# The first products of a GEGLU layer: three blocks of x by one transposing transfer, gate rows on ScalarE's queue

## The chip, the cores and the metric

The kernel runs on one core of a Trainium2 chip. The metric is the device time of one execution in microseconds, the median over runs; lower is better. The engines of the core are TensorE (PE, matrix products; PEld is its loading of weights), VectorE (DVE), ScalarE (ACT), GpSimd (POOL) and SyncE (SP). SyncE and ScalarE issue the transfers of this kernel, each on a queue of its own; sixteen DMA engines carry them.

## The reference

```python
B, S, D, F = 32, 32, 1024, 3584
# x [32, 32, 1024], w_gate and w_up [1024, 3584], w_down [3584, 1024], all bfloat16

def reference(x, w_gate, w_up, w_down):
    return (_gelu(x @ w_gate) * (x @ w_up)) @ w_down
```

`_gelu` is the tanh form of GELU. With x flattened, N = 1024 tokens go through a hidden width of F = 3584.

## The kernel before

A tile of 128 rows or columns is called a block. D has eight blocks (`DT`), F has 28 (`FT`), and tokens come in two halves of `NB` = 512. The eight blocks of D are cut in two halves of `KD` = 4, and these in two of `KQ` = 2. Both layers are computed by a scheme with seven products of half-sized matrices in place of eight, with sums and differences of quarters (`sums`, `t1` to `t4`) made on GpSimd and VectorE.

The quarter product that needs no sums is computed first, ahead of the rest, for 24 blocks of F (`NAHEAD`): the second half of x's columns times the lower half of the gate weights. Its moving operand is `b21` (x transposed: four blocks of D on the partitions, 512 tokens of the first half). Its weights come in six tiles `a12_ahead[i]`, each with four rows (blocks of D, index k) and four blocks of F (`KB`, index j). Tiles 0 and 1 are called a12a in the profile, tiles 2 to 5 a12b. A product for (i, j) sums over the four k into one accumulator of 128x512 in PSUM; `product_ahead` issues the matmuls for a range of k (line 290 in the profile). The finished accumulators are copied into `ahead_at` by ScalarE and VectorE (L348, L305).

Everything from `tc.manual_schedule()` on (line 191) is in an order written out by hand: each engine runs its instructions in the order of the code, and the tool that builds the kernel adds the waits. Transfers raise completion counters, eight of them used in turn; a transfer that reuses a counter waits for its previous user.

How x gets into `b21` is what the change is about. x lies in memory with tokens as rows, and `b21` needs it transposed:

- Block 0 of the four is loaded plainly into `x_nat` by SyncE (`load_nat`, L193), transposed on TensorE in four pieces (L266, function `transposed`), and copied from PSUM into `b21` by VectorE (L271).
- Block 1 is loaded plainly by ScalarE's queue and takes the same way through TensorE, between the products.
- Blocks 2 and 3 come by one transposing transfer on SyncE's queue (`load_xT`, L213). GpSimd's copy of one element (L221) from `x_nat` into `b21` is put ahead of it; the transfer overwrites that element, and so waits for the copy and with it for `x_nat`.

The rows of gate weights are issued by `load_ahead` (L206). On SyncE: row 0 of tile 0, row 0 of tile 1, rows 2 and 3 of tile 0 together, and, behind the transposing transfer, rows 2 and 3 of tile 1 together. On ScalarE: row 1 of tile 0 and row 1 of tile 1, behind a small read (`probe`, L202) and block 1 of x. After these SyncE issues tiles 2 and 3, the first chunks of the up and gate weights (L136), tile 4, the first half of x for both halves of the tokens, tile 5, and the last quarter of x.

TensorE starts with six products of constants (L254, `NWARM`), then transposes block 0 (L266), runs seven small products of constants (L275, `NFILL`), and then the products of tiles 0 and 1: row 0 of tile 0 in halves of 256 tokens (`by_halves(0)`), the transposes of block 1, row 0 of tile 1 for three of its four j, row 1 of tile 0 in halves, the remaining rows 0 and 1 of tile 1, and then rows 2 and 3 of both tiles, with the copies. Tiles 2 to 5 follow by `group_ahead`. Chunks of F (`for ci in range(NCH)`) and then the second layer take up the rest of the time.

Of the kernel before, what the change touches and what calls it, by code (L numbers as in the profile page):

```python
# [13 lines left out]
def kernel(  # L14
# [20 lines left out]
    nc = tc.nc  # L35
    P = nc.NUM_PARTITIONS
    fp32 = mybir.dt.float32
    f32r = mybir.dt.float32r
    bf16 = mybir.dt.bfloat16
# [3 lines left out]
    xf = x.flatten_outer_dims()  # L43
# [3 lines left out]
    NB = 512  # L47
    assert N == 2 * NB and D == 2 * NB and F % (4 * P) == 0
    DT, FT = D // P, F // P
    KD = DT // 2  # L50
# [4 lines left out]
    KQ = DT // 4  # L55
# [4 lines left out]
    KB = 4  # L60
# [12 lines left out]
    spool = one.enter_context(tc.tile_pool(name="s", bufs=2))  # L73
    xpool = one.enter_context(tc.tile_pool(name="x", bufs=1))
    ework = one.enter_context(tc.tile_pool(name="ework", bufs=2))
    ps1 = ctx.enter_context(tc.tile_pool(name="ps1", bufs=2, space=bass.MemoryType.PSUM))
# [29 lines left out]
    BANKS = {"A": 6, "C": 2}  # L106

    def acc(tag):
        return ps1.tile([P, NB], fp32, name=f"ps{tag}", tag=tag, bufs=BANKS[tag])
# [5 lines left out]
    b21 = xpool.tile([P, KD, NB], bf16, name="b21")  # L115
# [68 lines left out]
    ident = xpool.tile([P, P], bf16, name="ident")  # L184
    make_identity(nc, ident)
    NB_P = NB // P
    probe = xpool.tile([P // 4, KD, 2], bf16, name="probe")
    HALF = NB_P // 2
    x_nat = spool.tile([P, NB_P, KQ * P], bf16, name="x_nat", tag="s1")

    with tc.manual_schedule():
        def load_nat(eng, dt, p0, p1):
            eng.dma_start(  # L193
                out=x_nat[:, p0:p1, dt * P : (dt + 1) * P],
                in_=xf[p0 * P : p1 * P, (KD + dt) * P : (KD + dt + 1) * P].rearrange("(b p) d -> p b d", p=P),
            )

        assert KQ == 2
        load_nat(nc.sync, 0, 0, NB_P)


        nc.scalar.dma_start(out=probe, in_=wg_r[::4, KD:, :2])  # L202

        def load_ahead(i, k0, k1, eng=nc.sync, j0=0, j1=KB):
            f0 = i * KB
            eng.dma_start(  # L206
                out=a12_ahead[i][:, k0:k1, j0 * P : j1 * P],
                in_=wg_r[:, KD + k0 : KD + k1, (f0 + j0) * P : (f0 + j1) * P],
            )

        def load_xT(nb, d0, d1):
            t = ((b11, b12), (b21, b22))[d0 // KD][nb]
            nc.sync.dma_start_transpose(  # L213
                out=t[:, d0 % KD : (d1 - 1) % KD + 1, :], in_=xf[nb * NB : (nb + 1) * NB, d0 * P : d1 * P]
            )

        load_ahead(0, 0, 1)
        load_nat(nc.scalar, 1, 0, NB_P)
        load_ahead(1, 0, 1)
        load_ahead(0, KQ, KD)  # L220
        nc.gpsimd.tensor_copy(b21[:1, KQ, :1], x_nat[:1, 0, :1])  # L221
        load_xT(0, KD + KQ, DT)
        load_ahead(0, 1, KQ, nc.scalar)
        load_ahead(1, 1, KQ, nc.scalar)
        a12_ahead += [spool.tile([P, KD, KB * P], bf16, name="a12b", tag=t) for t in ("s2", "s4", "s1", "s3")]
        load_ahead(1, KQ, KD)
        def load_halves(i):
# [5 lines left out]
        for which in (1, 0):  # L233
            load_w_all(0, which)
        load_ahead(4, 0, KD)
        load_xT(0, 0, KD)
        load_xT(1, 0, KD)
        for j0 in range(0, KB, KB // 2):
            load_ahead(5, 0, KD, j0=j0, j1=j0 + KB // 2)
# [13 lines left out]
        for _ in range(NWARM):  # L253
            nc.tensor.matmul(warm_ps, lhsT=ones_w, rhs=ones_m, start=True, stop=True)  # L254

        def tp_tile(cols):
            return ps1.tile([P, cols], bf16, name="tp", tag="A", bufs=BANKS["A"])

        tps = [[tp_tile(HALF * P) for _ in range(2)]]
        whole_tp = tp_tile(NB_P * P)  # L260
        tps.append([whole_tp[:, h * HALF * P : (h + 1) * HALF * P] for h in range(2)])

        def transposed(dt):
            for half, tp in enumerate(tps[dt]):
                for b in range(HALF):
                    nc.tensor.transpose(  # L266
                        tp[:, b * P : (b + 1) * P], x_nat[:, half * HALF + b, dt * P : (dt + 1) * P], ident
                    )
            for half, tp in enumerate(tps[dt]):
                p0 = half * HALF * P  # L270
                nc.vector.tensor_copy(b21[:, dt, p0 : p0 + HALF * P], tp)  # L271

        transposed(0)
        for _ in range(NFILL):
            nc.tensor.matmul(warm_ps[:, :P], lhsT=ones_w, rhs=ones_w, start=True, stop=True)  # L275

# [11 lines left out]
        def product_ahead(ps, i, j, k0=0, k1=KD, cols=slice(None)):  # L288
            for k in range(k0, k1):
                nc.tensor.matmul(  # L290
                    ps[:, cols],
                    lhsT=a12_ahead[i][:, k, j * P : (j + 1) * P],
                    rhs=b21[:, k, cols],
                    start=(k == 0 and not cols.start),
                    stop=(k == KD - 1),
                    skip_group_check=True,
                )
# [32 lines left out]

        both = (nc.scalar.copy, nc.vector.tensor_copy)
        ps = [[acc(t) for t in tags] for tags in ("CCAA", "AAAA")]
        def by_halves(k):
            for half in range(2):
                for j in range(KB):
                    product_ahead(ps[0][j], 0, j, k, k + 1, slice(half * HALF * P, (half + 1) * HALF * P))

        by_halves(0)
        transposed(1)
        for j in range(KB - 1):  # L340
            product_ahead(ps[1][j], 1, j, 0, 1)
        by_halves(1)
        for j in range(KB):
            product_ahead(ps[1][j], 1, j, 0 if j == KB - 1 else 1, KQ)
        for i in (0, 1):
            for j in range(KB):
                product_ahead(ps[i][j], i, j, KQ)
# [26 lines left out]
        for ci in range(NCH):  # L374
# [7 lines left out]
            s1, s2, s3, s4 = ([s[:, :, fl * P : (fl + 1) * P] for fl in range(len(fts))] for s in s_tiles[ci])  # L382
# [87 lines left out]
        def halves(name, tags, dtype):  # L470
            return [late.tile([P, QF, NB], dtype, name=name, tag=t) for t in tags]

        def parts(two):

            return [two[b // 2][:, k0 % QF : (k1 - 1) % QF + 1, :] for b, (k0, k1) in enumerate(batches)]
# [15 lines left out]
        s1 = parts(halves("s1d", ("slo", "shi"), f32r))  # L491
# [103 lines left out]
        for h0, h1, upto in ((0, NB - P, NB - P), (NB - P, NB, NB)):  # L595
            cols = slice(h0, h1)
            ps = acc("C")[:, : h1 - h0]
# [33 lines left out]
```

## Time and profile before

| what | value |
|---|---|
| median of 3 runs | 273.57 us (272.9 to 273.75) |
| profiled execution, its own time | 273.33 us |
| profiled execution, span from first to last instruction | 271.4 us |
| mean granted TensorE clock | 1.000 |
| first transposing transfer: issue, landing after it | 3.44 us, 4.1 us |
| x's first and second block: landing after issue | 2.4 us, 3.3 us |
| gate rows of tiles 0 and 1, single: landing after issue | 3.1 to 3.8 us |
| first product of a gate row (L290) | 4.67 us on the chain |

Times inside the execution are microseconds from the start of the span. The chain of waits follows the work that ended last back to the start: at each step to what released it, or to the instruction before it on its engine. The timeline lists instructions in order of time, several of one line merged into one row ("x6"). A row "SPq" or "ACTq" is the issue of a transfer on SyncE's or ScalarE's queue; the time from its start to the landing of the data stands with the transfers. In a window's row the busy time of each engine is followed by granted clock, the share of the DMA engines' time and the rate in GB/s.

### The profile page before, as it was taken

How to read it: one execution, taken by the hardware profiler on the slowest of the kernel's cores; microseconds unless marked ns; L12 is line 12 of the kernel's file. 1: busy time of each engine (PE TensorE's matmuls, PEld its weight loads, DVE VectorE, ACT ScalarE, POOL GpSimd, SP SyncE). 2: the span in 40 equal slices, each digit the busy share in tenths (PEclk: the TensorE clock that was granted, in tenths of full speed). 3: DMA queues.
4: the chain of work that ended last, by engine and by line, in shares of the span. 5: the costliest groups of instructions: out<-in, count | busy, mean ns of one | idle time of the engine just before them, and what ended most of it. 6: DMA issues, size and time to landing. Idle time of an engine off the chain costs nothing.

```text
span 271.4 us, 3431 instructions
## 1 busy us (share of the span) xinstructions
PE 268.0 (99%) x1219; PEld 193.7 (71%) x1219; DVE 204.0 (75%) x205; ACT 115.4 (43%) x189; POOL 120.8 (45%) x61
## 2 busy tenths in 40 slices
PE   8999999999999999999999999999999999999996
PEld 5544776886787788688688687764458888888884
DVE  1447999986976877887777478469999999988711
ACT  2435756545644653645636535434000307870000
POOL 1080089997994994995995996000000000000000
PEclk9999999999999999999999999999999999999999
DMA  7999321514505505415234190005981537875111
GB/s 193 316 209 228 100 62 56 157 35 119 157 0 155 156 2 155 126 28 157 73 84 119 47 331 8 0 2 178 356 279 60 156 115 248 269 194 181 52 64 60
DMA packets 56657, 35.88 MB, mean 132 GB/s; under 512 B 10048, under 2 KB 56640, under 8 KB 56640
## 3 DMA queue, kind: packets, MB, share of 16 engines
q1 hardware_dynamic: 53232, 33.17, 43.3%
q10 hardware_dynamic: 3408, 2.49, 2.9%
q8 instruction: 10, 0.16, 0.3%
q14 instruction: 7, 0.06, 0.1%
HBM read 31.72 MB, written 2.10 MB: 125 GB/s over the span
## 4 chain that ended last, share of the span: by engine, by line
PE 99%; DVE 0%; issue 0%
PE psA L279 38%; PE psA L435 24%; PE psC L279 19%; PE psC L435 7%; PE psA L290 5%; PE psC L290 3%; PE psC L599 1%; PE psA L254 1%; PE psA L275 0%; PE tp L266 0%; DVE o_last L600 0%
## 5 line engine op out<-in xcount | busy, mean ns | idle before, releaser
L279 PE MATMUL psA<-t,s 128*128 128x512 f32 x224 | 57.2, 397 | 0.0
L246 ACT ACTIVATE h<-c 128x512 bf16<-128x512 f32 x56 | 34.4, 629 | 41.5 <-DVE c L309 41.5
L279 PEld LDWEIGHTS psA<-t,s 128*128 128x128 f32 x224 | 42.1, 188 | 9.5
L165 POOL TENSOR_TENSOR s<-wu 128x1024 fp32r<-128x1024 bf16 x13 | 29.5, 2271 | 28.0 <-DMA wu<-in_w_up_dram 24.0
L166 POOL TENSOR_TENSOR s<-s,wg 128x1024 fp32r<-128x1024 f32 x14 | 32.0, 2285 | 15.2 <-PE psA L279 14.2
L279 PE MATMUL psA<-b,wg 128*128 128x512 bf16 x128 | 29.4, 380 | 0.0
L168 POOL TENSOR_TENSOR s<-wg,wu 128x1024 fp32r<-128x1024 bf16 x13 | 28.9, 2219 | 0.0
L279 PE MATMUL psA<-t,a22r 128*128 128x512 f32 x112 | 27.9, 391 | 0.0
L279 PE MATMUL psC<-t,s 128*128 128x512 f32 x112 | 27.9, 391 | 0.0
L279 PE MATMUL psC<-b22r,s 128*128 128x512 f32 x112 | 27.7, 389 | 0.0
L309 DVE TENSOR_TENSOR c<-sn,psA 128x512 f32<-128x512 f32 x32 | 21.8, 682 | 6.7 <-PE psA L279 6.1
L314 ACT COPY sn<-psC 128x512 f32<-128x512 f32 x28 | 16.3, 588 | 22.8 <-PE psC L279 14.9
L279 PEld LDWEIGHTS psC<-t,s 128*128 128x128 f32 x112 | 21.0, 188 | 4.5
L279 PEld LDWEIGHTS psA<-t,a22r 128*128 128x128 f32 x112 | 21.0, 188 | 4.5
L279 PEld LDWEIGHTS psC<-b22r,s 128*128 128x128 f32 x112 | 21.0, 188 | 4.4
L309 DVE TENSOR_TENSOR c<-sn,psC 128x512 f32<-128x512 f32 x28 | 19.0, 686 | 6.0 <-PE psC L279 6.0
L412 DVE TENSOR_TENSOR lo<-c,h 128x512 bf16<-128x512 f32 x14 | 22.5, 1605 | 0.9
L279 PEld LDWEIGHTS <-wg 128*128 128x128 bf16 x128 | 11.8, 98 | 15.3 <-issue 2.4
L167 POOL TENSOR_TENSOR s<-wg,s 128x1024 fp32r<-128x1024 bf16 x10 | 21.6, 2160 | 0.8
L314 ACT COPY sn<-psA 128x512 f32<-128x512 f32 x32 | 18.3, 592 | 4.9 <-PE psA L279 4.6
L309 DVE TENSOR_TENSOR c<-ahead,psA 128x512 f32<-128x512 f32 x24 | 16.4, 686 | 3.5 <-PE psA L279 2.1
L412 DVE TENSOR_TENSOR hi<-c,h 128x512 bf16<-128x512 f32 x14 | 17.6, 1257 | 0.9
(88 smaller groups left out, 375.5 us busy)
## 6 DMA issues: line engine op xcount, KB each, us to landing
wu<-in_w_up_dram SPq DMA_DIRECT2D x14, 512.0 KB, 4.1
wdb<-in_w_down_dram SPq DMA_DIRECT2D x12, 512.0 KB, 4.8
wg<-in_w_gate_dram SPq DMA_DIRECT2D x10, 512.0 KB, 5.3
wdb<-in_w_down_dram SPq DMA_DIRECT2D x12, 384.0 KB, 4.5
v<-in_w_down_dram SPq DMA_DIRECT2D x4, 512.0 KB, 6.1
out_dram<-o_sb ACTq DMA_DIRECT2D x15, 128.0 KB, 1.7
v<-in_w_down_dram SPq DMA_DIRECT2D x4, 384.0 KB, 7.5
a12b<-in_w_gate_dram SPq DMA_DIRECT2D x4, 256.0 KB, 4.2
```

The source lines that it names most:

```text
L165: yield engs[0].tensor_tensor(s1, a21, a22, ADD)
L166: yield engs[1].tensor_tensor(s2, s1, a11, SUB)
L167: yield engs[2].tensor_tensor(s4, a12, s2, SUB)
L168: yield engs[3].tensor_tensor(s3, a11, a21, SUB)
L246: nc.scalar.activation(h, src, ACT.Gelu_apprx_tanh)
L254: nc.tensor.matmul(warm_ps, lhsT=ones_w, rhs=ones_m, start=True, stop=True)
L279: nc.tensor.matmul(ps, lhsT=lhs[:, k, :], rhs=rhs[:, k, :], start=(start and k == 0), stop=(k == KD - 1), skip_group_check=True,)
L290: nc.tensor.matmul(ps[:, cols], lhsT=a12_ahead[i][:, k, j * P : (j + 1) * P], rhs=b21[:, k, cols], start=(k == 0 and not cols.start), stop ...
L309: tt(t, s, ps, ADD)
L314: nc.scalar.copy(t, ps)
L412: tt(g_of(ft)[:, NB:], added(sn5[fl], psa[fl]), h1[fl], MUL)
L435: nc.tensor.matmul(banks[m], lhsT=lhs(k)[:, m * P : (m + 1) * P], rhs=rhs(k), start=(start and k == 0), stop=(k == HF - 1), skip_group_che ...
```

## The change

Block 0 of x takes the way that it had. Block 1 no longer goes through TensorE: the transposing transfer now brings blocks 1, 2 and 3 together, is issued right behind block 0 on SyncE's queue, and GpSimd's copy ahead of it is gone. ScalarE's queue has the single rows 0 and 1 of tiles 0 and 1, in turn, and then rows 2 and 3 of tile 0 one by one; only rows 2 and 3 of tile 1 stay on SyncE. TensorE's order becomes: row 0 of tile 0 in halves, row 0 of tile 1, row 1 of tile 0 in whole rows of 512 tokens, row 1 of tile 1, and from there as before.

```diff
-    x_nat = spool.tile([P, NB_P, KQ * P], bf16, name="x_nat", tag="s1")
+    x_nat = spool.tile([P, NB_P, P], bf16, name="x_nat", tag="s1")
...
-        load_nat(nc.sync, 0, 0, NB_P)
+        nc.sync.dma_start(out=x_nat, in_=xf[:NB, KD * P : (KD + 1) * P].rearrange("(b p) d -> p b d", p=P))
         nc.scalar.dma_start(out=probe, in_=wg_r[::4, KD:, :2])
...
-        load_ahead(0, 0, 1)
-        load_nat(nc.scalar, 1, 0, NB_P)
-        load_ahead(1, 0, 1)
-        load_ahead(0, KQ, KD)
-        nc.gpsimd.tensor_copy(b21[:1, KQ, :1], x_nat[:1, 0, :1])
-        load_xT(0, KD + KQ, DT)
-        load_ahead(0, 1, KQ, nc.scalar)
-        load_ahead(1, 1, KQ, nc.scalar)
+        load_xT(0, KD + 1, DT)
+        for k in range(KD):
+            for i in range(2 if k < KQ else 1):
+                load_ahead(i, k, k + 1, nc.scalar)
...
-        transposed(0)
+        tps = [ps1.tile([P, HALF * P], bf16, name="tp", tag="A", bufs=BANKS["A"]) for _ in range(2)]
+        for half, tp in enumerate(tps):
+            for b in range(HALF):
+                nc.tensor.transpose(tp[:, b * P : (b + 1) * P], x_nat[:, half * HALF + b, :], ident)
+            nc.vector.tensor_copy(b21[:, 0, half * HALF * P : (half + 1) * HALF * P], tp)
...
-        by_halves(0)
-        transposed(1)
-        for j in range(KB - 1):
-            product_ahead(ps[1][j], 1, j, 0, 1)
-        by_halves(1)
-        for j in range(KB):
-            product_ahead(ps[1][j], 1, j, 0 if j == KB - 1 else 1, KQ)
+        for half in range(2):
+            for j in range(KB):
+                product_ahead(ps[0][j], 0, j, 0, 1, slice(half * HALF * P, (half + 1) * HALF * P))
+        for k in range(KQ):
+            for i in range(k == 0, 2):
+                for j in range(KB):
+                    product_ahead(ps[i][j], i, j, k, k + 1)
```

More of the change, by code (lines that the diff above doesn't have):

```diff
@@ L188 @@
     HALF = NB_P // 2
-    x_nat = spool.tile([P, NB_P, KQ * P], bf16, name="x_nat", tag="s1")
+    x_nat = spool.tile([P, NB_P, P], bf16, name="x_nat", tag="s1")
     with tc.manual_schedule():
[L192 to L196, printed above, removed]
         assert KQ == 2
-        load_nat(nc.sync, 0, 0, NB_P)
+        nc.sync.dma_start(out=x_nat, in_=xf[:NB, KD * P : (KD + 1) * P].rearrange("(b p) d -> p b d", p=P))
         nc.scalar.dma_start(out=probe, in_=wg_r[::4, KD:, :2])
@@ L209, in load_ahead, with load_xT @@
             )
-        def load_xT(nb, d0, d1):
+        def load_xT(nb, d0, d1, eng=nc.sync):
             t = ((b11, b12), (b21, b22))[d0 // KD][nb]
-            nc.sync.dma_start_transpose(
+            eng.dma_start_transpose(
                 out=t[:, d0 % KD : (d1 - 1) % KD + 1, :], in_=xf[nb * NB : (nb + 1) * NB, d0 * P : d1 * P]
             )
-        load_ahead(0, 0, 1)
-        load_nat(nc.scalar, 1, 0, NB_P)
-        load_ahead(1, 0, 1)
-        load_ahead(0, KQ, KD)
-        nc.gpsimd.tensor_copy(b21[:1, KQ, :1], x_nat[:1, 0, :1])
-        load_xT(0, KD + KQ, DT)
-        load_ahead(0, 1, KQ, nc.scalar)
-        load_ahead(1, 1, KQ, nc.scalar)
+        load_xT(0, KD + 1, DT)
+        for k in range(KD):
+            for i in range(2 if k < KQ else 1):
+                load_ahead(i, k, k + 1, nc.scalar)
         a12_ahead += [spool.tile([P, KD, KB * P], bf16, name="a12b", tag=t) for t in ("s2", "s4", "s1", "s3")]
@@ L254 @@
             nc.tensor.matmul(warm_ps, lhsT=ones_w, rhs=ones_m, start=True, stop=True)
[L256 to L271, printed above, removed]
-        transposed(0)
+        tps = [ps1.tile([P, HALF * P], bf16, name="tp", tag="A", bufs=BANKS["A"]) for _ in range(2)]
[3 more added lines that the diff above has]
+            nc.vector.tensor_copy(b21[:, 0, half * HALF * P : (half + 1) * HALF * P], tp)
         for _ in range(NFILL):
@@ L332 @@
         ps = [[acc(t) for t in tags] for tags in ("CCAA", "AAAA")]
-        def by_halves(k):
-            for half in range(2):
-                for j in range(KB):
-                    product_ahead(ps[0][j], 0, j, k, k + 1, slice(half * HALF * P, (half + 1) * HALF * P))
-        by_halves(0)
-        transposed(1)
-        for j in range(KB - 1):
-            product_ahead(ps[1][j], 1, j, 0, 1)
-        by_halves(1)
-        for j in range(KB):
-            product_ahead(ps[1][j], 1, j, 0 if j == KB - 1 else 1, KQ)
+        for half in range(2):
[3 more added lines that the diff above has]
+            for i in range(k == 0, 2):
+                for j in range(KB):
+                    product_ahead(ps[i][j], i, j, k, k + 1)
         for i in (0, 1):
```

## The prediction

> **What bounds the kernel now.** I read the busy shares first, then the chain of work that ended last, then the chain's first 13 us in order of time. The page says (sections 1 and 4):
>
> ```profile
> PE 268.0 (99%) x1219; PEld 193.7 (71%) x1219; DVE 204.0 (75%) x205; ACT 115.4 (43%) x189; POOL 120.8 (45%) x61
> PE 99%; DVE 0%; issue 0%
> ```
>
> TensorE is busy for 268.0 of 271.4 us, and the chain is TensorE alone: it waits for nobody. So an edit can gain only what it takes off TensorE, and can lose whatever it makes TensorE wait for. The start of that chain (start, duration, what):
>
> ```profile
> 0.77 2.72 PE psA L254 x6
> 3.49 0.43 PE tp L266 x4
> 3.92 0.75 PE psA L275 x7
> 4.67 0.43 PE psC L290 x2
> 5.09 0.40 PE psA L290 x2
> 5.49 0.22 PE psC L290 x2
> 5.71 0.22 PE psA L290 x2
> 5.93 0.22 PE tp L266 x4
> 6.15 0.65 PE psA L290 x3
> ...
> 8.75 0.86 PE psC L290 x4
> 9.62 2.59 PE psA L290 x12
> ```
>
> Each piece ends where the next begins. Every input of this stage lands in time, but with how much to spare? For that I read the timeline, which gives the issues, and then the transfers issued in short windows, which give issue to landing:
>
> ```profile
> 0.74 0.45 SPq L193 DMA_DIRECT2D x_nat<-in_x_dram  x1
> 1.20 0.45 ACTq L193 DMA_DIRECT2D x_nat<-in_x_dram  x1
> 1.24 1.48 SPq L206 DMA_DIRECT2D a12a<-in_w_gate_dram  x3
> 3.44 1.34 SPq L213 DMA_TRANSPOSE b<-in_x_dram  x1
> 4.35 1.29 PEld L290 LDWEIGHTS <-a12a 128*128 128x128 bf16 x8
> ```
>
> ```profile
> b<-in_x_dram SPq DMA_TRANSPOSE x1, 4.1
> b<-in_x_dram SPq DMA_TRANSPOSE x1, 8.7
> b<-in_x_dram SPq DMA_TRANSPOSE x1, 5.0
> b<-in_x_dram SPq DMA_TRANSPOSE x1, 5.5
> ```
>
> The four transposing transfers stand in order of issue (3.44, 11.06, 16.24 and 20.39 us): the first has two blocks of x, the others four. The first lands at 3.44 + 4.1 = 7.54; TensorE first reads it at 8.75, 1.2 us later. The first gate row of tile 0 lands at 1.24 + 3.1 = 4.34, and its weights load at 4.35.
>
> Last, the windows of the stage (the columns at the end of a row are granted clock, DMA share and GB/s):
>
> ```profile
> 5.40:6.00 0.60, 0.60 (x10) 0.56 (x9) 0.00 (x0) 0.00 (x0) 0.00 (x0) 1.00 1.35 317
> 6.00:6.40 0.40, 0.40 (x5) 0.19 (x3) 0.21 (x2) 0.00 (x0) 0.00 (x0) 1.00 0.95 176
> 14.50:18.00 3.50, 3.50 (x18) 1.58 (x17) 1.43 (x3) 1.17 (x2) 3.42 (x2) 1.00 1.18 219
> ```
>
> The DMA engines are full. While the first transposing transfer moves, the rate falls to 176 GB/s for a time; around the second, which ran behind gate rows on its queue, it is 219 GB/s over 3.5 us. Plain rows alone have 322 GB/s (4.00 to 5.00).
>
> **What the change takes off the path.** The four L266 transposes of x's second block: 0.22 us (the row at 5.93). Tile 0's second row was multiplied in eight halves, 0.88 us (6.80 to 7.67: four pairs of 0.22); now in four whole rows of 2.59/12 = 0.216 each, 0.86. The same columns, counted as no gain. Two DVE copies of 0.29, GpSimd's copy of one element (0.18) and x's second plain transfer go as well, none of them on the chain. **Gain: 0.22 us**, and no more.
>
> **What it moves.** On SyncE the order becomes: x's first block (0.74 to 1.19), the transfer of three blocks at 1.24 with no wait before it, the last two rows of tile 1, then tile 2. The issue of the transfer took 1.34 us for two blocks and 2.93 for four at best (16.24 to 19.17), so about 2.1 for three: SyncE goes on at 3.3 instead of 4.83. On ScalarE stand the probe and six single gate rows, each about 0.49 to issue: 1.20, 1.69, 2.2, 2.7, 3.2; the sixth (tile 0, row 3) waits for the counter of the first row, some 4.3. Behind that wait ScalarE has only its table load (1.28) and the activation of one column (0.21), done by about 6.3; its next work was at 9.22, so this costs nothing (cover 2.9 us).
>
> First inputs. x's first block keeps its issue. The first gate row now leads ScalarE's queue; x's second block took 3.3 from that place, which would be 1.20 + 3.3 = 4.50; the best is the 2.4 of x's first block, 3.6. Its first matmul runs at 4.67, behind the fill of L275, so neither bound adds or gains anything; taken as 0.
>
> **The term that decides: when do the three blocks land?** TensorE needs them after the eight halves (5.93) and the four rows of tile 1's first step (4 x 0.216): at 6.79, and not at 8.75, since row 1 of x comes by this transfer now. Bounds for the landing:
> - Below: no contention. Between 4.1 (two blocks) and 5.0 (four), 4.55 for three: 1.24 + 4.55 = 5.8. No wait. Earlier than needed brings nothing, as TensorE has no gap.
> - Above: like the second transfer, 8.7: 9.9, a wait of 3.15 us.
> - Between: in the same time ScalarE's queue brings five gate rows of 131 KB. With 393 KB of x that is 1.05 MB, from about 2.9 us, when x's first block is through. At 219 GB/s this takes 4.8 us, to 7.7; the first transfer landed some 0.65 us after its last small packets (about 6.9), so 8.35: a wait of 1.56 us. At 261 GB/s (the mean of 5.40 to 7.50) it is 4.0 us, landing 7.55, a wait of 0.76.
>
> I take 219 GB/s: its window is the nearest to a transposing transfer amid gate rows through its whole course.
>
> The Trainium skill, "DMA: Bandwidth & Descriptors", section "Issuing engines are not separate DMA queues", says that transfers from different issuing engines run on the same 16 DMA engines and interleave, so a second queue saves issue time alone. The trace agrees: both queues together moved 304 GB/s from 3.00 to 4.00, SyncE's alone 345 from 8.00 to 9.00. That page's table "Latency and other measured facts" gives 261 GB/s for a transposing transfer; by that figure the wait would be the estimate of 0.76 above, and the time 273.9.
>
> **Sum.** 273.33 (the profiled execution: span 271.4 and 1.9 around it) - 0.22 + 1.56 = **274.7 us**. The median of the runs shown is 273.57, 0.24 above that execution, so the sum is 0.4% over the median.
>
> What is late next: in the changed order tile 2's second half waits, on SyncE, for the counter that the transposing transfer raises (before, that of a gate row): its issue goes from 5.95 to about 8.4, and behind it queue tiles 3 and 4, the first up and gate chunks and the other blocks of x. Tile 2's second half is read at 12.21 + 0.43 + 1.3 = 13.9, and 8.4 + 4.5 (its issue to landing before) is 12.9: covered. The tightest later: the last four blocks of x land at 25.9, DVE's L361 runs 25.96 to 28.25, and TensorE reads its result at 29.44, 1.2 us later. TensorE itself comes 1.3 later, so a delay of up to 2.5 is covered; beyond that it is paid one for one.
>
> **Rivals.**
> - *It lands in time* (not slower). ScalarE's rows come spaced by 0.49 us, and a queue of small packets may get more turns than one of large: read in stretches of 0.2 us, from 2.80 to 3.40 ScalarE's queue moved 317 small packets (81 KB) beside 53 large ones (53 KB) of SyncE's. With 60% of the bytes, the transfer's 393 KB go with 262 KB of rows: 0.655 MB at 261 GB/s is 2.5 us, to 5.4, landing 6.05, before 6.79. Then 273.33 - 0.22 = 273.1. It decides from a landing at 6.79. Against it: the slow stretches inside every transposing transfer (176 GB/s above; 44 from 18.50 to 19.00).
> - *It lands as late as the second one did*, 8.7 after issue: 273.1 + 3.15 = 276.3. For it: that transfer too had gate rows beside it. Against: most of its time it stood behind 512 KB on its own queue.
> - *The pace of TensorE doubles later.* The same pair of halves took 0.43 at 4.67 and 0.22 at 5.49, so TensorE runs at half pace until about 5.1, 4.3 us after its first matmul, though the granted clock reads 1.00. If x's first block or the first gate row comes late enough to open a gap before 5.1 and the rise is put off by as long again, 4.3 us of work at half pace cost 2.15: 275.3. For it: the first row was on time by 0.01 us before. Against: x's first block was there 0.35 us before 3.49, and the fill covers the row. "TensorE: Matmul & The Clock Gate", Part 1, in the Trainium skill, puts the rise after about 3.4 us of sustained work; by that the price is an estimate of 1.7.
>
> **How the numbers follow.** Forecast 0.52 (its own range 273.9 to 275.3), in time 0.29, like the second one 0.08, late pace 0.07, something unnamed 0.04. A measurement of this kernel can tell about 0.3%, 0.8 us, from no change; against the profiled execution that is 274.15, a landing at 7.83. Of the forecast 0.42 lies beyond it; with 0.08, 0.07 and 0.02 that makes slower 0.59. Same: 0.10 of the forecast, 0.25 of in time, 0.02. Faster: 0.04, by scatter alone (the runs shown spread over 0.85 us), as only 0.22 can be gained. Range 273.0 to 276.0: it holds the in-time case and the late pace, and leaves out the third.
>
> **What would show it.** Right: in the changed trace TensorE stands idle before the whole rows of tile 0's second step (near 6.8 us), for 0.8 to 2 us, released by the transposing transfer, whose landing is 6.5 to 7.5 us after its issue; one run of L266 instead of two; no other gap. Wrong: no idle time there, or a landing under 5.5 us; an idle time before 5.1, or pairs of 0.43 after it; a gap at the weights of tile 2 or at L361's result.

## The result and the profile after

The changed kernel takes 275.13 us (median of 6, 274.78 to 276.83) against 273.66 before (median of 6, 272.9 to 274.0): a ratio of 1.0065 (of the means), 95% interval 1.0037 to 1.0094, so slower, by 1.5 us between the medians. The profiled execution took 274.94 us, with a span of 273.2. The page's busy shares and the shares of the chain, in the changed kernel:

```profile
PE 267.8 (98%) x1198; PEld 192.9 (71%) x1211; DVE 204.2 (75%) x203; ACT 115.5 (42%) x189; POOL 119.8 (44%) x60
PE 95%; DMA 3%; issue 0%; ACTq 0%; DVE 0%
```

For the first time transfers stand in the chain. (TensorE's busy time reads 0.2 us less than before, but 13 of its matmuls are missing from this trace: 1198 beside 1211 weight loads, so what the change took off is read below from starts.) Where they stand is read in the chain's first 16 us in order of time:

```profile
1.21 3.05 DMA a12a<-in_w_gate_dram
4.26 0.02 issue
4.28 6.20 DMA a12a<-in_w_gate_dram
10.48 0.05 issue
10.52 0.82 PE psC L265 x3
```

From 10.52 on it is TensorE alone, as before. The chain follows only the wait that ended last, a gate row's; the waits ahead of it are in the timeline of the changed kernel (a tile's first, second and fourth row are rows 0, 1 and 3 of the code; in brackets the idle time before the instruction and what ended it; L265 is the L290 of the kernel before):

```profile
5.74 1.65 PE L265 MATMUL psA<-b,a12a 128*128 128x256 bf16 x6
6.34 0.55 PEld L265 LDWEIGHTS <-a12a 128*128 128x128 bf16 x4 [0.46 <-DMA a12a<-in_w_gate_dram]
7.90 0.10 PEld L265 LDWEIGHTS <-a12a 128*128 128x128 bf16 x1 [1.01 <-DMA a12a<-in_w_gate_dram]
8.15 0.59 PE L265 MATMUL psC<-b,a12a 128*128 128x512 bf16 x2 [0.76 <-DMA b<-in_x_dram]
10.52 0.82 PE L265 MATMUL psC<-b,a12a 128*128 128x512 bf16 x3 [0.27 <-DMA a12a<-in_w_gate_dram]
13.77 0.59 PE L265 MATMUL psC<-b,a12b 128*128 128x512 bf16 x2
```

The first product of tile 2 (a12b) starts at 13.77; before it started at 12.04. So 1.73 us of the loss are complete here. A matmul is drawn longer than its share of the array, so the sum goes by starts (a whole row occupies 0.216, a half 0.11):

| what | us |
|---|---|
| the last half of tile 0's first row starts at 5.94, before at 5.66: TensorE's pace doubled later | +0.28 |
| transposes of x's second block are gone | -0.22 |
| tile 1's first row: halves end at 6.05, its products start at 6.35 | +0.30 |
| tile 0's second row: tile 1's products end at 7.22, the next start at 8.15; the row lands at about 7.9, the transposing transfer at 8.1 | +0.93 |
| tile 0's fourth row: the product before it ends at 10.08, the next starts at 10.52 | +0.44 |
| sum | +1.73 |

The transfers explain the three waits. Issue to landing in the changed kernel: the transposing transfer (issued at 1.24), tile 0's first row (1.21) and tile 1's first (1.7):

```profile
b<-in_x_dram SPq DMA_TRANSPOSE x1, 6.9
a12a<-in_w_gate_dram ACTq DMA_DIRECT2D x1, 128.0 KB, 3.0
a12a<-in_w_gate_dram ACTq DMA_DIRECT2D x1, 128.0 KB, 4.5
```

The four rows behind these took 5.6, 5.6, 6.3 and 6.2; before, no single row took more than 3.8. The windows of the changed kernel (the last three columns: granted clock, DMA share, GB/s):

```profile
3.00:4.00 1.00, 1.00 (x9) 0.71 (x8) 0.26 (x2) 0.00 (x0) 0.00 (x0) 1.00 0.79 140
4.00:5.00 1.00, 1.00 (x10) 0.87 (x8) 0.24 (x2) 0.36 (x1) 0.00 (x0) 1.00 1.05 168
5.00:6.00 1.00, 1.00 (x7) 0.62 (x5) 0.00 (x0) 0.99 (x2) 0.00 (x0) 1.00 1.28 184
6.00:7.00 1.00, 0.87 (x5) 0.31 (x4) 0.00 (x0) 0.14 (x1) 0.00 (x0) 1.00 1.17 177
7.00:8.00 1.00, 0.39 (x2) 0.10 (x1) 0.00 (x0) 0.00 (x0) 0.00 (x0) 1.00 1.12 311
```

The DMA engines are about as full as before (share 0.79 to 1.28 in the four windows from 3.00 to 7.00, before 1.01 to 1.24), but for four microseconds they move 140 to 184 GB/s where the kernel before had 304 from 3.00 to 4.00 and 322 from 4.00 to 5.00. From 7.00, when the transposing transfer's last packets have moved, the rate is 311.

### The profile page after: what moved, and what is told of

It reads as the page before. It is cut to its first block, busy times and chain, and to the rows that moved or that the text cites. A ratio compares the mean times of both kernels' runs of the same rounds, so it can differ in the third digit from the quotient of the medians.

```text
span 273.2 us, 3395 instructions
## 1 busy us (share of the span) xinstructions
PE 267.8 (98%) x1198; PEld 192.9 (71%) x1211; DVE 204.2 (75%) x203; ACT 115.5 (42%) x189; POOL 119.8 (44%) x60
## 4 chain that ended last, share of the span: by engine, by line
PE 95%; DMA 3%; issue 0%; ACTq 0%; DVE 0%
PE psA L254 38%; PE psA L405 24%; PE psC L254 19%; PE psC L405 7%; PE psA L265 4%; DMA a12a<-in_w_gate_dram 3%; PE psC L265 2%; PE psC L569 1%; ACTq L194 0%; DVE o_last L570 0%
## 5 line engine op out<-in xcount | busy, mean ns | idle before, releaser
L254 PE MATMUL psA<-b,wg 128*128 128x512 bf16 x119 | 27.8, 379 | 0.6
```

What stands on the lines that cost most here:

```text
L254: nc.tensor.matmul(ps, lhsT=lhs[:, k, :], rhs=rhs[:, k, :], start=(start and k == 0), stop=(k == KD - 1), skip_group_check=True,)
```

## The experiments

The question was whose fault the 4 us at half rate are: the transfer's early start, its third block, the six rows on one queue, or the two kinds side by side. The theory was the last; each run changes one of the others.

**Three blocks, held back.** GpSimd's copy is put back, so that the transfer starts after x's first block has landed.

```diff
+        nc.gpsimd.tensor_copy(b21[:1, 1, :1], x_nat[:1, 0, :1])
         load_xT(0, KD + 1, DT)
```

> The changed kernel, but the transfer of three blocks is held until x's first block has landed, as the kernel before held its two (GpSimd's copy of one element put ahead of it). Theory (a transposing transfer and plain gate rows that move at the same time slow each other, so an early start costs the rows): the gate rows that are through before the transfer's first packets, some 5.4 us, land 3 to 4 us after issue as in the kernel before (3.1 to 3.8), not 4.5 to 6.3; TensorE no longer waits near 6.3 for tile 1's first row; the transfer, issued at 3.4, lands 4.6 to 5 later, 8.0 to 8.5, so one wait of 0.8 to 1.3 us for it stays; time 274.2 to 275.0. Rival 1 (six rows on one queue are late by themselves): rows as late as in the changed kernel, the waits of 0.30 and 0.44 us stay, time 275.0 to 276. Rival 2 (three blocks take 6.9 us from issue whatever runs beside them): landing at 10.3, time 276.5 to 277.5.

Measured: 278.28 us, ratio 1.0172 (1.0144 to 1.0201). The rows before the transfer's packets did land 2.8 to 3.4 after issue, and TensorE didn't wait for tile 1's first row; so six rows on one queue are not late by themselves. But the transfer, beside the last two rows, took 6.3 us, not 4.6 to 5, and one of those rows 5.9. TensorE waited 3.06 us for it, and then the windows of this run show what such a wait brings (first column of numbers behind the window: its length, then TensorE's busy time):

```profile
8.00:8.80 0.80, 0.00 (x0) 0.00 (x0) 0.00 (x0) 0.00 (x0) 0.00 (x0) 1.00 1.33 202
9.00:9.20 0.20, 0.00 (x0) 0.00 (x0) 0.00 (x0) 0.00 (x0) 0.00 (x0) 0.50 1.16 131
9.96:14.00 4.04, 4.04 (x10) 1.43 (x11) 0.00 (x0) 0.00 (x0) 0.00 (x0) 0.50 1.12 338
```

The granted clock fell to half at about 9.0, some 2 us after the last matmul, and stayed there until 15.8: tile 2 started at 18.01, 5.97 later than before, about half of it by the wait and half by the clock. The time was far outside what the theory gave (274.2 to 275.0); an early start is better than a late one with the same rows on the other queue. The time lies nearer to that of the second rival, three blocks that take 6.9 us whatever runs beside them; that one is decided further down, where the rows are taken away.

**Two blocks, early and held.** Here x's second block goes back to its plain transfer and to TensorE, and TensorE's order is that of the kernel before. The rows stay on ScalarE. The diff is that of the second run against the kernel before; the first run also drops GpSimd's copy, so that its transfer starts early.

```diff
-        load_ahead(0, 0, 1)
-        load_nat(nc.scalar, 1, 0, NB_P)
-        load_ahead(1, 0, 1)
-        load_ahead(0, KQ, KD)
+        load_nat(nc.sync, 1, 0, NB_P)
         nc.gpsimd.tensor_copy(b21[:1, KQ, :1], x_nat[:1, 0, :1])
         load_xT(0, KD + KQ, DT)
-        load_ahead(0, 1, KQ, nc.scalar)
-        load_ahead(1, 1, KQ, nc.scalar)
+        for k in range(KD):
+            for i in range(2 if k < KQ else 1):
+                load_ahead(i, k, k + 1, nc.scalar)
```

> The kernel before, with its two plain blocks of x on SyncE, right behind them the transposing transfer of two blocks with no wait before it, and all single gate rows on ScalarE as in the changed kernel; TensorE's order is that of the kernel before. Theory (the early transposing transfer and the rows slow each other): rows land 4 to 6 us after issue, TensorE waits 0.5 to 1.2 us for the second row of tile 0 (needed at about 6.6), though the transposing transfer itself, needed at 8.75, is in time; time 274.2 to 275.2. Rival 1 (rows late because of one queue): the same 274.2 to 275.2 here, and as much in the run that holds the transfer. Rival 2 (only the third block in the transfer is at fault, landing after it is needed): 273.4 to 273.9, no wait.

> As the run with two blocks early, but the transposing transfer is held by GpSimd's copy until x's first block has landed, so only the gate rows' queue and the place of x's second plain block differ from the kernel before. Theory (the early start is at fault): rows land 3 to 4 us after issue, no wait of TensorE over 0.2 us, time 273.3 to 274.0. Rival 1 (one queue for the rows is at fault): rows at 4.5 to 6.3 after issue and the time 274.2 to 275.2.

Measured: early 275.33 us, ratio 1.0056 (1.0037 to 1.0074); held 274.04, ratio 1.0025 (1.0012 to 1.0038), both just above the ranges given. Early, the transfer took 5.7 and the rows 3.6 to 5.5; held, 4.7 and 3.3 to 3.8. So two blocks meet the same trouble when they start early, and the third block alone is not at fault; and six rows on ScalarE's queue are not late when the transfer starts behind them. Where the early run loses its time is only half shown. Its executions fall in two groups, four at 274.1 and five at 275.3 to 275.9, and the profiled one (274.13) is of the first. There tile 2 started 0.82 us late: 0.44 since tile 0's first row landed at 4.8, beside x's second block on the other queue, and 0.38 since the pace doubled near 6.6; at the second row, where the theory put the wait, TensorE lost nothing. The held run has 0.48 of the same two kinds (the first product at 4.70, the pace at 6.1).

**No row beside the transfer.** Two measurements. In the first ScalarE reads an element of the transfer's result before it issues any row. In the second all rows are issued by SyncE, right behind the transfer, on its own queue.

```diff
         load_xT(0, KD + 1, DT)
+        held = xpool.tile([1, 1], bf16, name="held")
+        nc.scalar.copy(held, b21[:1, 1, :1])
```

```diff
-                load_ahead(i, k, k + 1, nc.scalar)
+                load_ahead(i, k, k + 1)
```

> A measurement: the changed kernel, but ScalarE reads one element that the transposing transfer of three blocks brings before it issues any gate row, so no gate row moves on the other queue while the transfer is under way. Theory (they slow each other): the transfer lands 4.4 to 5.2 us after its issue (6.9 in the changed kernel), at 5.6 to 6.4. Rival 2 (three blocks take that long by themselves): 6.5 to 7.2 after issue. The rows start some 4.5 us later, so the time is 278 to 282 in both; that says nothing.

> A measurement: the changed kernel with all six single gate rows on SyncE's queue, right behind the transposing transfer, so that ScalarE's queue carries the probe alone. Theory (plain packets of the other queue beside it are at fault): the transfer lands 3.7 to 4.6 us after issue, each row 3.2 to 4.3. Rival (any plain packets near it): the transfer at 6 to 7, the rows at 4.5 to 6.3. TensorE's first product waits for the first row, some 6.5 us, in both, so the time is 275 to 279 and says nothing.

Measured: the transfer of three blocks, issued at 1.24 as in the changed kernel, landed 3.9 us after issue in both, in the first earlier than the 4.4 to 5.2 expected (times 279.50 and 275.07 us, one execution each). Of the second of these runs, the transfer, the first row behind it and the third:

```profile
b<-in_x_dram SPq DMA_TRANSPOSE x1, 3.9
a12a<-in_w_gate_dram SPq DMA_DIRECT2D x1, 128.0 KB, 3.1
a12a<-in_w_gate_dram SPq DMA_DIRECT2D x1, 128.0 KB, 3.0
```

The edit changes nothing but the queue that carries the rows, and the transfer takes 3.9 in place of 6.9, the rows 2.9 to 3.5 in place of 3.0 to 6.3. That clears the start and the third block: what slows the transfer is the plain rows of the other queue, which move at the same time. It doesn't show that rows of its own queue would do no harm beside it, since here they come after it: the first is issued at 3.01 (1.21 in the changed kernel), and counted in stretches of 0.25 us SyncE's queue moves 283, 285 and 274 packets from 3.75 to 4.5, and the first two packets of a row are in the last of these. Whether it takes the other queue, or only the overlap in time, stays open.

**Rows ahead of the transfer, or behind it.** Three ways to keep the early transfer of three blocks and part the rows from it: four rows ahead of it, on both queues; row 0 of both tiles on ScalarE and the rest behind it on SyncE; everything on SyncE, row 0 of both tiles ahead.

```diff
+        load_ahead(0, 0, 1)
+        load_ahead(1, 0, 1)
+        for i in range(2):
+            load_ahead(i, 1, KQ, nc.scalar)
         load_xT(0, KD + 1, DT)
+        load_ahead(0, KQ, KD)
```

```diff
         load_xT(0, KD + 1, DT)
+        for i in range(2):
+            load_ahead(i, 0, 1, nc.scalar)
+        for i in range(2):
+            load_ahead(i, 1, KQ)
+        load_ahead(0, KQ, KD)
```

```diff
+        for i in range(2):
+            load_ahead(i, 0, 1)
         load_xT(0, KD + 1, DT)
+        for i in range(2):
+            load_ahead(i, 1, KQ)
+        load_ahead(0, KQ, KD)
```

(In each, the changed kernel's loop over six rows is taken out.)

> The changed kernel with the gate rows moved so that the first four are ahead of the transposing transfer of three blocks: row 0 of both tiles on SyncE between x's first block and the transfer, row 1 of both on ScalarE, rows 2 and 3 of both on SyncE behind the transfer. Theory (it is slow only beside plain transfers of the other queue): the four rows land within 4.2 us of issue, the transfer, issued at 2.2, within 4.5 us (6.2 to 6.7, needed at about 6.8); waits of TensorE before 12 us at most 0.3 us together; time 273.0 to 273.9. Rival (three blocks are always too late for the second step of tile 0, wherever the rows are): a wait of 0.8 us or more, 274.3 or more.

> The changed kernel with its transfer of three blocks left where it is (issued at 1.24, right behind x's first block, no wait), but row 1 of both tiles and rows 2 and 3 of tile 0 moved from ScalarE to SyncE behind it; only row 0 of both tiles stays on ScalarE. Theory (plain packets of the other queue beside the transfer are at fault, those behind it on its own queue are not): the transfer lands 4 to 5 us after issue (5.2 to 6.2, not 8.1), row 1 of tile 0, issued at 3.1, lands at 6.6 to 7.1, waits of TensorE at most 0.5 us together, time 273.0 to 274.0. Rival (an early transposing transfer is at fault with any rows near it): the transfer at 6.5 to 7 after issue and the rows 5 us and more, time 274.8 or more.

> The run with the rows behind the transfer again, for the profile of a typical execution: 11 of its 12 executions so far took 273.3 to 275.0, the profiled one 276.6. Theory: in such an execution tile 1's first row, the only one on ScalarE's queue that meets the transfer, lands within 4.4 us of its issue (5.6 in the profile so far), the transfer within 5.6 (6.5), and TensorE waits at most 0.8 us before 12 us. Rival (the transfer is as slow in every execution, and the times differ for another reason): 5.4 or more and 6.3 or more again.

> The changed kernel's transfer of three blocks with every gate row on SyncE's queue: row 0 of both tiles ahead of it, the rest behind it; ScalarE's queue carries the probe alone. Theory (only plain packets of the other queue slow the transfer, and it them): the transfer, issued at 2.2, lands within 4.2 us (by 6.4, needed at about 6.8), the rows 2.9 to 4 after issue, row 1 of tile 0 at about 6.9; waits of TensorE at most 0.4 us; time 273.1 to 273.9, no slower than the kernel before by more than 0.3%, and too little is to be gained (0.22 us) to be told apart as faster. Rival (three blocks cost over 0.8 us in any order): 274.3 or more.

Measured, first way: 274.14 us, ratio 1.0035 (1.0023 to 1.0048). The transfer took 4.6, the rows 3.2 to 3.6, and TensorE's one wait in this stage was the transfer's:

```profile
6.88 0.59 PE L267 MATMUL psC<-b,a12a 128*128 128x512 bf16 x2 [0.29 <-DMA b<-in_x_dram]
```

In the profile tile 2 started at 12.05, as before the change (12.04), but 0.19 of that is luck: the pace doubled earlier, at about 4.9, and the halves were through at 5.57 (before 5.76). The median was still outside the range given (273.0 to 273.9). The profiled execution (273.79) was one of the faster of eight; what the others lost in addition no profile shows.

Second way: 274.01 us, ratio 1.0032 (1.0014 to 1.0051), at the edge of what was expected in the time, and beside it in the transfers. One row on the other queue (row 0 of tile 1; that of tile 0 was all but through) was enough to slow the transfer, in the first profile and in the second:

```profile
b<-in_x_dram SPq DMA_TRANSPOSE x1, 6.5
b<-in_x_dram SPq DMA_TRANSPOSE x1, 6.1
```

In the first profile (276.59 us, the slowest of twelve) the row took 5.6, and both figures are those of the rival; in the other (274.21 us) it took 5.0, and both lie in between what the two theories gave for it. So the transfer's 6 us alone don't make the time of the first. From 4.75 to 6.25 in the first profile SyncE's queue moved 81 to 184 packets in each 0.25 us, nearly all of the transfer, while ScalarE's moved 3 to 7. The rows behind the transfer on its own queue took 4.2 to 4.8, so row 1 of tile 0 landed at 8.1 and 7.7, not at 6.6 to 7.1. In the first profile the clock went down as well, after a wait of 2.2 us:

```profile
7.00:7.20 0.20, 0.00 (x0) 0.00 (x0) 0.00 (x0) 0.00 (x0) 0.00 (x0) 1.00 0.89 256
7.60:10.00 2.40, 2.40 (x7) 0.78 (x6) 0.00 (x0) 0.00 (x0) 0.00 (x0) 0.50 1.10 347
```

Third way: 274.84 us, ratio 1.0046 (1.0029 to 1.0064). The transfers did what the theory said (the transfer 4.3, in time at 6.5; the rows 2.5 to 3.9), the time did not; it is in the rival's range (274.3 or more), though the wait is a row's and not the transfer's. With one queue for all, row 1 of tile 0 was issued at 4.08, behind the 1.79 us that SyncE spent on the issue of the transfer, and landed at 7.7 (about 6.9 was expected), when TensorE had been idle for more than a microsecond; in the profile (276.37 us, the slowest of eight) tile 5 was late as well:

```profile
7.70 0.61 PE L267 MATMUL psC<-b,a12a 128*128 128x512 bf16 x2 [1.20 <-DMA a12a<-in_w_gate_dram]
26.33 1.90 PE L267 MATMUL psC<-b,a12b 128*128 128x512 bf16 x8 [1.20 <-DMA a12b<-in_w_gate_dram]
```

So none of the three beats the kernel before.

**The changed kernel again.**

> The changed kernel again, for a second profile beside the two above. Both theories: 274.8 to 275.4. If the 0.28 us by which TensorE's pace doubled later is part of the change, the doubling stands at 5.9 us again; if it falls by chance, it stands anywhere from 5.2 to 6.4, as in the runs so far, which do the same work until then.

Measured: 275.86 us, ratio 1.0118 (1.0077 to 1.0158), above the range given: three of six executions took 276.8 to 278.4, and their mean granted clock was 0.993 to 0.994, where the others had 0.999 and more (the longest of the first six, 276.83 us, had 0.994). In the profile (274.71 us) the transfer took 6.6, the rows behind the first 4.9 to 6.3, and tile 2 started at 13.54, with the same three waits, the one at tile 1's first row 1.0 us this time. The pace doubled near 5.2 here, not at 5.9.

## Why the prediction was right

**The gain** of 0.22 us, and no more, held: the four transposes are gone from the sequence of starts, and the products take the time that they took.

**The deciding term** was the landing of three blocks, put at 8.35 by a rate of 219 GB/s; it was 8.1. That the two lie so near is in part luck, since three terms were off and nearly cancel. The rate was lower (140 to 184 from 3 to 7 us). But of the 0.59 MB that moved from 3.0 to 6.5 the transfer had 0.39, two thirds, so that its last packets moved before 7.0, not at 7.7, with most of the rows still behind it. And it landed 1.1 us or more after them, not 0.65. The two bounds are both seen now: 3.9 after issue without rows beside it (4.55 was taken), 6.9 with them.

**The wait was mis-shared.** All 1.56 us were charged to the transfer at tile 0's second row; there it was 0.93, and the row itself, landing at 7.9, would have cost some 0.7 of it had the transfer been in time. The other 0.74 stood at two rows that the prediction had on time: tile 1's first (0.30) and tile 0's fourth (0.44). The contention was counted against the transfer only; rows that took 3.1 to 3.8 were expected to take that again and took 4.5 to 6.3. "No other gap" among the signs was wrong for this reason, and the sum came out right (1.34 forecast, 1.61 between the two profiled executions, 1.47 between the medians) because one shared delay was paid at three places in place of one: 1.67 us of waits against 1.56. The 0.28 of the late pace, below, is in the measured loss by chance.

**The rival "in time"** had the share about right (60%, measured two thirds), but not the rate: it took 261 GB/s for the two together, and even with one row on the other queue the transfer took 6.1 and 6.5. **The rival "as late as the second one"** (8.7) was not reached. **The late pace** happened (5.9, and by the starts about 5.3 before, where 5.1 was read), but not by the mechanism put forward: no gap lay ahead of 5.9, and the same kernel doubled its pace at 5.2 in the other profile. So the 0.28 us are put down to the execution, not to the change.

**What was to be covered** was: ScalarE's table load behind its waiting row, tile 2's second half, and L361's result (L331 after the change), ready at 29.61 and read at 31.16.

The rule of the Trainium skill, "DMA: Bandwidth & Descriptors", section "Issuing engines are not separate DMA queues", that transfers of different issuers share the same engines and interleave, agrees with the rows, but is only half of what decided: the two together moved 140 to 184 GB/s in the windows from 3 to 7 us, less than the two in turn on one queue (199 to 266) and than rows and x's plain block on both queues (304 and more). The 261 GB/s that the table "Latency and other measured facts" on that page of the Trainium skill gives for a transposing transfer would have put the wait, as an estimate, at 0.76.

## What to carry to other kernels

In this stage a transposing transfer and plain transfers of another queue should not move at the same time: each made the other up to 3 us later, though the transfer alone, or both in turn on one queue, was quick. So try to order them in time (plain rows that are needed first go ahead, as in the kernel before) before spreading them over queues, and price contention against both sides. Ordering has its own price: what stands behind a transposing transfer on its queue is issued 1.8 us later, and no order tried here beat the kernel before. When TensorE waits for nothing, a fraction of a microsecond taken off it is all that can be won, while the loads behind it can cost several.

## What was not expected of the hardware

- The rate of the DMA engines with a transposing transfer on one queue and plain rows on the other: 129 to 196 GB/s from 3 to 7 us in the first profile with a single such row beside it, with a share of 0.89 to 1.26; transfer and rows in turn on one queue moved at 199 to 266. Why, the traces don't show.
- TensorE's granted clock fell to 0.50 about 2 us after its last matmul, in two profiles (waits of 3.06 and 2.2 us); waits of 0.93 and 1.20 us left it at 1.00. It stayed down from 8.97 to 15.80 in the one and from 7.21 to 10.63 in the other, so for 6.83 and 3.42 us, twice the same length and once. The mean clock of the two executions, 0.988 and 0.994, is what two such stretches and one give (half of 6.83 in 277.5 us is 1.2%, half of 3.42 in 274.5 is 0.6%). So 0.994 in the late executions of the changed kernel fits one such stretch, worth up to 1.7 us; no profile shows their waits.
- TensorE's pace doubled at different times in different executions, after the same work up to about 3.4 us: at 3.8 in the first profile with a row behind, 4.6 with one queue, 4.9 with four rows ahead, and 5.2 to 6.6 in seven others (in the two left it falls into or behind a long wait). While TensorE works, half of such a difference is what it is worth: up to 1.4 us between two profiles of this case, nearly as much as the change cost.
